# A second buffer for the raw keys of an attention job

## The chip, the cores and the metric

The kernel runs on one core of one Trainium2 chip. The metric is the device time of one execution in microseconds (us), lower is better. Engines of the core are named as the profile names them: PE (TensorE, matrix products; PEld is its weight load), DVE (VectorE), ACT (ScalarE), POOL (GpSimd) and SP (SyncE, which here only issues DMAs; "SPq" marks its DMA instructions). Each engine works through its own list of instructions in order; semaphores hold an instruction back until what it reads is there and what it overwrites is no longer needed.

## What is computed

Three stages follow one another: causal attention with a decay, and two feed-forward layers with a gate of their own kind. Cut to what matters:

```python
def _attn_ref(q, k, v, f):                 # (4, 8, 576, 64), f (4, 8, 576)
    scores = scale * np.matmul(q, k.transpose(0, 1, 3, 2))
    cum = np.cumsum(np.log(np.clip(f, 0.0001, 1.0)), axis=-1)
    decay = cum[:, :, :, None] - cum[:, :, None, :]
    scores = np.where(causal, -1000000000.0, scores + decay)
    ...                                    # softmax over the keys
    return np.matmul(attn, v)

def _moe_ref(x, w_in, w_out):              # 2304 tokens, 512 -> 2048 -> 512
    h = x @ w_in
    return (h * np.clip(h + 3.0, 0.0, 6.0) / 6.0) @ w_out

def _moe2_ref(x, w_in, w_out):
    h = x @ w_in
    g = np.where(h >= 1, h, np.where(h <= -1, 0.0, (h + 1) ** 2 / 4.0))
    return g @ w_out
```

## The kernel before

**Attention** is cut into 64 jobs, 16 for each of the four batches. A pair of heads takes one job for its first 256 queries (a job "two": two heads, two tiles of 128 queries) and three for the remaining 320 (two jobs "one", one head and two tiles each, and a job "last" that takes the last 64 queries of both heads). For each job `u_load` issues its DMAs, `u_split` prepares its operands, `u_scores` makes the scores of a tile on PE and the softmax on DVE and ACT, `u_norm` divides by the row sum, `u_trans` transposes the probabilities on PE (tile `pt`) and `u_out` multiplies with the values (`av`) and writes the result as the first layer's input `xt`.

**The raw keys.** The first eight jobs use keys and queries as they come. From the ninth on (`n >= NATS`) a job of kind "two" or "one" loads its keys into `kraw` (two DMAs, line 259, one for each half of the partitions, the same keys in both) and its queries into `qraw` (lines 264, 272 and 273). `u_split` then makes `kk` from `kraw`: ACT rounds all of it (the helper at line 121) and DVE subtracts the rounded part in the lower 64 partitions (the helper at line 129). In the same way `qraw` becomes `qh` (ACT) and `ql` (DVE). There are 40 such jobs. `kraw` and `qraw` each had one buffer: the next job's DMAs wait until DVE has made `kk` and `ql` of the job before. `kk`, `qh` and `ql` have three buffers each. The decay row `dec` of a job (lines 288 and 239, broadcast from `ncum` in DRAM) has two.

**The feed-forward layers** run over 9 blocks of 256 tokens in the first layer and 5 blocks of up to 512 in the second; for each block 16 chunks of the hidden width. `moe_h` makes `hp` (line 561), ACT and DVE make `u` and from it `g` in two parts (rounded part on ACT at line 121, rest on DVE at line 129), `moe_o` adds to `o` (line 608 in the first layer, 615 in the second). The weights come as pairs of 32-bit words (`wraw`, line 157), are decoded by ACT (line 178) and DVE (lines 179, 183, 186, 189) into `wr`, which has two buffers, and are written to DRAM as `wf` (by POOL's DMA queue, line 194) or split into `w`; `w` is read back from `wf` (line 160).

**Order.** The first layer's steps begin while the attention still runs, and pieces of attention are put between its steps by a table of costs. The program text is not yet the order: the framework's scheduler orders each engine's instructions by a simulation of its own, where a tile's free buffer is one of the conditions, and sets the semaphores. Eight semaphores serve the DMAs of SP in turn, so that a DMA also waits for the one eight places ahead of it.

Of the kernel before, what the change touches and what calls it, by code (L numbers as in the profile page):

```python
# [8 lines left out]
F32 = mybir.dt.float32  # L9
# [5 lines left out]
B, H, S, D = 4, 8, 576, 64  # L15
NT, DM, DFF = B * S, H * D, 2048
P = 128
# [57 lines left out]
def tile_kernel(  # L75
# [34 lines left out]
    att = att_cm.__enter__()  # L110
# [120 lines left out]
    def u_load(n):  # L231
# [13 lines left out]
        if d["nat"]:  # L245

            kk = att.tile([P, S], F32, tag="kk", name="kn", bufs=3)
            qq = att.tile([P, 2 * QA], F32, tag="qh", name="qn", bufs=3)
            nc.sync.dma_start(out=kk[:, 0:nk], in_=k[b, h:h + 2, :, 0:nk].rearrange("h p n -> (h p) n"))
            for y in range(2):  # L250
                nc.sync.dma_start(
                    out=qq[y * D:(y + 1) * D, 0:nq], in_=q[b, h + y, y * D:(y + 1) * D, q0:q0 + nq]
                )
            d.update(kk=kk, qh=qq)
        else:
            kraw = att.tile([P, S], F32, tag="kraw", name="kraw", bufs=1)
            qraw = att.tile([P, 2 * QA], F32, tag="qraw", name="qraw", bufs=1)
            for y in range(2):
                nc.sync.dma_start(
                    out=kraw[y * D:(y + 1) * D, 0:nh * nk].rearrange("p (h n) -> p h n", h=nh),  # L260
                    in_=k[b, h:h + nh, :, 0:nk].rearrange("h p n -> p h n"),
                )
            if kind == "two":
                nc.sync.dma_start(
                    out=qraw.rearrange("p (h n) -> p h n", h=nh),
                    in_=q[b, h:h + nh, :, q0:q0 + nq].rearrange("h p n -> p h n"),
                )
            else:

                o = QA + W4 * (h % 2)  # L270
                nc.gpsimd.memset(qraw[:, S - o:S - o + W4], 0.0)
                nc.sync.dma_start(out=qraw[:, 0:QA], in_=q[b, h, :, q0:q0 + QA])
                nc.sync.dma_start(out=qraw[:, o:o + W4], in_=q[b, h, :, q0 + QA:S])
            d.update(kraw=kraw, qraw=qraw)
# [213 lines left out]
    def attention_pieces():  # L488
# [4 lines left out]
        for n in range(nu + 2):  # L493
            ready = []
            if n < nu:
                d = jobs[n]
                tl = d["tiles"]
                for i in tl:
                    def sc(n=n, i=i, tl=tl):
                        u_scores(n, i)  # L500
                        if i == tl[0] and n + 1 < nu:
                            u_split(n + 1)
                        if i == tl[-1]:
                            u_norm(n)
                            if n + 2 < nu:
                                u_load(n + 2)
                    w = min(i * P + P, S)
                    ready.append(((4 if d["kind"] == "two" else 2) * max(110, w * 0.45), sc))
# [221 lines left out]
    logs(lf)  # L730
    seq, ends = attention_pieces()
    u_load(0)
    u_split(0)
    weights_ahead(-1)
    u_load(1)
    after = cumulative(lf)
    pos = 0
# [112 lines left out]
```

## Time and profile before

| | |
|---|---|
| median of 3 runs | 1085.44 us (1082.84 to 1087.59) |
| the profiled execution | 1085.11 us |
| its span, from the first to the last instruction | 1083.4 us |
| mean granted TensorE clock | 0.974 of full speed |
| busy: PE, PEld | 1034.3 us (95%), 903.9 us (83%) |
| busy: DVE, ACT, POOL | 591.8 us (55%), 541.5 us (50%), 89.8 us (8%) |
| chain that ended last | PE 69%, DMA 15%, DVE 7%, issue 4%, ACT 4% |

Busy time is the time in which an engine executed; the share is that of the span. The attention jobs fill the stretch up to about 560 us, together with the first layer; from then on there are the feed-forward layers alone. In a row of the timeline the first number is the start in us from the span's start, the second how long the instruction (or the run of equal ones) took, and the bracket at the end says how long the engine had been idle ahead of it and what ended that wait.

### The profile page before, as it was taken

The numbers are of one execution on the slowest core, as the hardware profiler recorded it, in microseconds if no ns is written. First come the engines' busy times: TensorE is split into PE (matmuls) and PEld (weight loads), VectorE is DVE, ScalarE is ACT, GpSimd is POOL, SyncE is SP. The second block draws the span as 40 slices with busy tenths as digits, with TensorE's granted clock in tenths as the row PEclk, the third lists the DMA queues.
The fourth block names the chain that finished last, engine by engine and source line by source line (L and its number), as shares of the span: only waits on it lengthen the run. The fifth ranks groups of instructions, "written<-read, shape, count | busy, mean of one in ns | idle before, by whom it ended". The sixth has DMA issues, their size and how long they took to land.

```text
span 1083.4 us, 18101 instructions
## 1 busy us (share of the span) xinstructions
PE 1034.3 (95%) x6556; PEld 903.9 (83%) x6556; DVE 591.8 (55%) x1510; ACT 541.5 (50%) x1330; POOL 89.8 (8%) x223
## 2 busy tenths in 40 slices
PE   7987999989799989999999999999999999999998
PEld 5776989979688889888989999888888888888887
DVE  7999984766577776777653436422422322332232
ACT  6877755656456655556553235533333333333343
POOL 2200010111021111121101000000100100000000
PEclk8688999999999999999999999999999999999999
DMA  8976681783586686864826035200200200010010
GB/s 235 337 222 185 213 299 54 226 277 111 182 282 197 202 298 185 282 212 123 249 68 253 2 96 167 90 1 1 77 1 1 72 6 1 19 39 1 1 40 20
DMA packets 69785, 144.20 MB, mean 133 GB/s; under 512 B 11584, under 2 KB 38720, under 8 KB 65600
## 3 DMA queue, kind: packets, MB, share of 16 engines
q1 hardware_dynamic: 67136, 134.66, 39.6%
q0 software_dynamic: 2560, 8.39, 2.0%
q8 instruction: 51, 0.84, 0.3%
q14 instruction: 38, 0.31, 0.1%
HBM read 116.74 MB, written 26.29 MB: 132 GB/s over the span
## 4 chain that ended last, share of the span: by engine, by line
PE 69%; DMA 15%; DVE 7%; issue 4%; ACT 4%; SPq 1%; POOL 0%; DVEq 0%; ACTq 0%; POOLq 0%
PE hp L561 31%; PE o L608 12%; PE o L615 10%; PE ps L615 8%; DMA qraw<-in_q 5%; DMA dec<-ncum 3%; PE pt L432 3%; DMA kraw<-in_k 2%; PE av L474 2%; DMA wraw<-in_w 2%; PE sc L388 1%; DMA x2d<-osb 1%; DMA wf<-wr 1%; DVE prob L339 1%; DVE wr L186 1%
## 5 line engine op out<-in xcount | busy, mean ns | idle before, releaser
L608 PE MATMUL o<-g,w 128*128 128x256 f32 x1728 | 250.3, 289 | 16.8 <-ACT g L121 15.3
L561 PE MATMUL hp<-xt,w 128*128 128x256 f32 x1728 | 250.6, 292 | 7.8 <-ACT w L121 5.1
L608 PEld LDWEIGHTS o<-g,w 128*128 128x128 f32 x1728 | 225.9, 191 | 26.7 <-ACT g L121 19.2
L561 PEld LDWEIGHTS hp<-xt,w 128*128 128x128 f32 x1728 | 226.8, 194 | 14.5 <-ACT w L121 6.1
L561 PE MATMUL hp<-x,w 128*128 128x512 f32 (+1 forms) x960 | 211.4, 369 | 0.0
L561 PEld LDWEIGHTS hp<-x,w 128*128 128x128 f32 x960 | 169.1, 188 | 32.5
L572 DVE SCALAR_TENSOR_TENSOR u<-hp,u 128x512 f32<-128x512 f32 (+1 forms) x80 | 50.8, 637 | 195.9 <-ACT u L571 195.9
L129 DVE TENSOR_TENSOR g<-u,g 128x256 fp32r<-128x256 f32 (+1 forms) x224 | 112.8, 505 | 71.5 <-ACT g L121 71.1
L121 ACT ACTIVATE g<-u 128x256 fp32r<-128x256 f32 (+1 forms) x224 | 106.1, 475 | 88.4 <-DVE u L572 55.3
L570 ACT ACTIVATE u<-hp 128x512 f32<-128x512 f32 (+1 forms) x80 | 44.6, 557 | 173.3 <-PE hp L561 171.5
L615 PE MATMUL o<-w,g 128*128 128x512 f32 x480 | 125.0, 396 | 0.0
L615 PEld LDWEIGHTS o<-w,g 128*128 128x128 f32 x480 | 89.1, 188 | 19.9
L345 ACT ACTIVATE prob<-prob,mx 128x512 f32<-128x512 f32 (+4 forms) x144 | 83.5, 581 | 37.4 <-DVE mx L339 37.0
L615 PE MATMUL ps<-w,g 128*128 128x512 f32 x384 | 100.4, 396 | 0.0
L568 DVE SCALAR_TENSOR_TENSOR u<-u,hp 128x256 f32<-128x256 f32 x144 | 59.4, 416 | 53.8 <-ACT u L567 53.2
L567 ACT ACTIVATE u<-hp 128x256 f32<-128x256 f32 x144 | 53.8, 378 | 67.2 <-PE hp L561 65.4
L615 PEld LDWEIGHTS ps<-w,g 128*128 128x128 f32 x384 | 72.3, 188 | 17.4
L432 PE MATMUL pt<-ident,prob 128*128 128x128 f32 (+1 forms) x400 | 69.1, 296 | 12.6 <-DVE prob L417 12.1
L339 DVE CUSTOM_DVE_ANT_0 prob<-sc,dec 128x256 f32<-128x256 f32 (+1 forms) x112 | 58.8, 533 | 25.1 <-PE sc L388 11.9
L121 ACT ACTIVATE pt<-pt 128x512 f32<-128x512 f32 (+3 forms) x160 | 61.9, 433 | 18.7 <-PE pt L432 18.2
L432 PEld LDWEIGHTS pt<-ident,prob 128*128 128x128 f32 (+1 forms) x400 | 50.3, 150 | 18.4 <-DVE prob L417 12.8
L178 ACT ACTIVATE wr<-wraw 128x512 f32<-128x512 f32 x64 | 43.0, 671 | 44.5 <-DMA wf<-wr 19.0
(76 smaller groups left out, 975.5 us busy)
## 6 DMA issues: line engine op xcount, KB each, us to landing
wraw<-in_w SPq DMA_DIRECT2D x64, 512.0 KB, 6.4
w<-wf SPq DMA_DIRECT2D x24, 1024.0 KB, 8.5
dec<-ncum SPq DMA_DIRECT2D x45, 256.0 KB, 6.6
kraw<-in_k SPq DMA_DIRECT2D x64, 144.0 KB, 3.8
wf<-w SPq DMA_DIRECT2D x8, 1024.0 KB
wf<-wr POOLq DMA_DIRECT2D x32, 256.0 KB, 6.0
w<-wf SPq DMA_DIRECT2D x16, 512.0 KB, 4.1
vv<-in_v SPq DMA_DIRECT2D x16, 320.0 KB, 10.6
```

The source lines that it names most:

```text
L121: nc.scalar.activation(out=out, in_=in_, func=AF.Copy)
L129: e.tensor_tensor(out=out, in0=in_, in1=hi.bitcast(F32), op=ALU.subtract)
L339: nc.vector.tensor_tensor_reduce(out=py[:, a:e], in0=s, in1=dc, scale=-0.125, scalar=mx[:, 2 * z:2 * z + 1] if x else 3.0e38, op0=ALU.add, ...
L345: nc.scalar.activation(out=py, in_=py, func=AF.Exp, scale=-1.0, bias=mx[:, 2 * z + x:2 * z + x + 1], accum_out=sm[:, z:z + 1],)
L432: nc.tensor.transpose(t[:nk, o:o + P], p[:, c:c + nk], ident)
L561: nc.tensor.matmul(hp, lhsT=ws[:, a, k], rhs=x[:, bb, 0:w], start=(k == 0 and a == 0 and bb == 0), stop=(k == KD - 1 and bb == 1),)
L567: nc.scalar.activation(out=u, in_=hp, func=AF.Relu, bias=3.0, scale=1.0)
L568: nc.vector.scalar_tensor_tensor(out=u, in0=u, scalar=6.0, in1=hp, op0=ALU.min, op1=ALU.mult)
L570: nc.scalar.activation(out=u, in_=hp, func=AF.Relu, bias=0.5, scale=0.5)
L572: nc.vector.scalar_tensor_tensor(out=u, in0=hp, scalar=1.0, in1=u, op0=ALU.max, op1=ALU.min)
L608: nc.tensor.matmul(o, lhsT=ws[:, a, KD + k], rhs=gg[:, bb], start=False, stop=(n == NCH - 1 and bb == 1 and k % 2 == 1),)
L615: nc.tensor.matmul(acc[j][k], lhsT=gg[:, bb, k * P:(k + 1) * P], rhs=ws[:, a, KD:2 * KD].rearrange("p k n -> p (k n)"), start=(n == 0 and ...
```

## The change

One number: `kraw` gets two buffers in the pool `att` instead of one, 2304 bytes more in each partition.

```diff
-            kraw = att.tile([P, S], F32, tag="kraw", name="kraw", bufs=1)
+            kraw = att.tile([P, S], F32, tag="kraw", name="kraw", bufs=2)
             qraw = att.tile([P, 2 * QA], F32, tag="qraw", name="qraw", bufs=1)
```

No instruction is added or taken away. The scheduler, which sees the free buffer, puts the instructions of SP, ACT, DVE and PE into another order. The first difference on SP lies in the first 20 us, on ACT and DVE at the eighth job with raw keys, on PE some 200 us into the span. In the rows that follow, a line with + stands in the new program alone, one with - in the old alone, and a number behind a name tells one buffer's use from another's.

The first place is the loads of two neighbouring jobs "one", about 450 to 470 us into the span before. On SP (`kraw_6613` with `qraw_6614` is a job's load, `kraw_6656` with `qraw_6657` the next job's, `kraw_6935` that of the job after):

```order
 L273 DMA qraw_6614<-in_q 128x64
-L157 DMA wraw_6944<-in_w 128x1024
-L259 DMA kraw_6613<-in_k 64x576
+L259 DMA kraw_6656<-in_k 64x576 x2
+L259 DMA kraw_6935<-in_k 64x576
 L160 DMA w3_118<-wf15_97 128x2048
-L259 DMA kraw_6613<-in_k 64x576
+L259 DMA kraw_6935<-in_k 64x576
 L157 DMA wraw_6946<-in_w 128x1024
+L157 DMA wraw_7226<-in_w 128x1024
+L239 DMA dec_6445<-ncum_114 128x1x576
 L272 DMA qraw_6657<-in_q 128x256
```

The keys of each job stand one job earlier in SP's queue, and the decay row `dec_6445` now stands ahead of the next job's queries.

On DVE at the same place (`ql_6645` belongs to the queries `qraw_6614`, `wr_6865` to a weight chunk, `prob1_6434` is the last reader of the buffer into which `dec_6445` is loaded):

```order
-L129 TENSOR_TENSOR ql_6645<-qraw_6614,qh_6644 128x384
+L186 SCALAR_TENSOR_TENSOR wr_6865<-wraw_6683,wr_6865 128x512
+L189 SCALAR_TENSOR_TENSOR wr_6865<-wraw_6683,wr_6865 128x512
 L339 ISA prob1_6434,mx_6308<-sc_6435,dec_6277 128x256
 L339 ISA mx_6308 128x1
-L179 TENSOR_SCALAR wr_6865<-wr_6865 128x512
 L568 SCALAR_TENSOR_TENSOR u_6425<-u_6425,hp_6412 128x256
 L339 ISA prob0_6459,mx_6400<-sc_6460,dec_6320 128x256
 L339 ISA mx_6400 128x1
-L183 TENSOR_SCALAR wr_6865<-wr_6865 128x512
+L129 TENSOR_TENSOR ql_6645<-qraw_6614,qh_6644 128x384
```

The split of the queries has moved from ahead of `prob1_6434` to behind it, and the weight steps of `wr_6865` have moved ahead.

The second place is DVE some 15 us later, between the softmax of the job "last" and the two divisions (line 417) whose results PE transposes next:

```order
-L179 TENSOR_SCALAR wr_7175<-wr_7175 128x512
+L129 TENSOR_TENSOR kk_6726<-kraw_6656,kk_6726 64x576
+L186 SCALAR_TENSOR_TENSOR wr_7175<-wraw_6944,wr_7175 128x512
+L129 TENSOR_TENSOR kk_6988<-kraw_6935,kk_6988 64x576
 L408 RECIPROCAL rd_6608<-sum_6399 128x2
-L129 TENSOR_TENSOR kk_6726<-kraw_6656,kk_6726 64x576
-L183 TENSOR_SCALAR wr_7175<-wr_7175 128x512
+L568 SCALAR_TENSOR_TENSOR u_6700<-u_6700,hp_6687 128x256
+L189 SCALAR_TENSOR_TENSOR wr_7175<-wraw_6944,wr_7175 128x512
+L408 RECIPROCAL rd_6652<-sum_6473 128x1
+L179 TENSOR_SCALAR wr_7182<-wr_7182 128x512
 L417 TENSOR_SCALAR prob0_6459<-prob0_6459,rd_6608 128x384
```

Two keys' splits instead of one, both steps of the weight decoding and `u_6700` now stand ahead of the divisions.

The third place is ACT about 456 us into the span, where a row sum (`sum_6045`) is needed by the next divisions:

```order
 L121 ACTIVATE kk_6392<-kraw_6313 128x576
 L178 ACTIVATE wr_6576<-wraw_6410 128x512
+L121 ACTIVATE kk_6643<-kraw_6613 128x576
 L407 ACTIVATE sum_6045<-sum_6045 128x2
```

The rounding of the next job's keys, which stood some twenty instructions further on, now stands ahead of the row sum. At eleven places ACT now rounds two jobs' keys one directly behind the other, where before it never did.

## Rows read from the trace of the kernel before

**Rows 1.** Busy time by stretch: us, busy (x count), PEclk, DMA share, GB/s

```profile
216.00:560.00 344.00, 323.02 (x2449) 292.19 (x2449) 239.27 (x712) 200.52 (x571) 51.59 (x138) 0.98 0.66 210
560.00:680.00 120.00, 120.00 (x967) 115.43 (x964) 55.20 (x113) 47.78 (x107) 5.68 (x10) 1.00 0.37 125
```

**Rows 2.** PE's waits, 216 to 560 us: total us, times, longest

```profile
PE pt L432 <- DVE prob L417: 10.2, 6, 3.6
PE o L608 <- ACT g L121: 6.6, 5, 2.8
```

**Rows 3.** ACT's waits for raw queries and keys, whole span: total, times, longest

```profile
ACT qh L121 <- DMA qraw<-in_q: 20.2, 10, 3.4
...
ACT kk L121 <- DMA kraw<-in_k: 14.7, 9, 4.4
```

**Rows 4.** Instructions on tile kraw: count, duration in ns min/median/max

```profile
L259 SPq DMA_DIRECT2D kraw<-in_k x80: 465/587/1231, 14.4 to 542.4; - x80
L121 ACT ACTIVATE kk<-kraw x40: 615/674/702, 39.6 to 551.6; 128x576 fp32r<-128x576 f32 x32, 128x512 fp32r<-128x512 f32 x8
L129 DVE TENSOR_TENSOR kk<-kraw,kk x40: 689/755/841, 41.0 to 552.4; 64x576 fp32r<-64x576 f32 x32, 64x512 fp32r<-64x512 f32 x8
```

**Rows 5.** Timeline of DVE, ACT and PE, 478 to 484 us

```profile
478.57 0.69 DVE L339 CUSTOM_DVE_ANT_0 prob<-sc,dec 128x512 f32<-128x512 f32 x1 [2.29 <-DMA dec<-ncum]
...
481.55 0.68 ACT L121 ACTIVATE kk<-kraw 128x576 fp32r<-128x576 f32 x1 [4.40 <-DMA kraw<-in_k]
...
482.27 0.76 DVE L129 TENSOR_TENSOR kk<-kraw,kk 64x576 fp32r<-64x576 f32 x1 [1.57 <-ACT kk L121]
...
483.40 0.81 DVE L417 TENSOR_SCALAR prob<-prob,rd 128x384 f32<-128x384 f32 x2
...
483.87 0.44 PE L432 MATMUL pt<-ident,prob 128*128 128x128 f32 x2 [2.27 <-DVE prob L417]
```

**Rows 6.** Busy time by stretch, just behind that stall (columns as in rows 1)

```profile
485.00:488.40 3.40, 3.40 (x17) 3.36 (x16) 3.37 (x9) 2.48 (x7) 1.52 (x4) 0.51 0.24 79
```

**Rows 7.** Timeline of DVE and SP, 464 to 467 us

```profile
464.93 0.56 DVE L129 TENSOR_TENSOR ql<-qraw,qh 128x384 fp32r<-128x384 f32 x1 [3.80 <-ACT qh L121]
465.41 0.69 DVE L339 CUSTOM_DVE_ANT_0 prob<-sc,dec 128x512 f32<-128x512 f32 x1
...
466.37 0.55 SPq L239 DMA_DIRECT2D dec<-ncum  x1
```

**Rows 8.** DVE's weight steps by line, whole span: busy us, mean ns

```profile
L189 DVE SCALAR_TENSOR_TENSOR wr<-wraw,wr 128x512 int32<-128x512 int32 x64 | 44.3, 692 | 0.4
L186 DVE SCALAR_TENSOR_TENSOR wr<-wraw,wr 128x512 int32<-128x512 int32 x64 | 43.8, 686 | 0.2
...
L183 DVE TENSOR_SCALAR wr<-wr 128x512 int32<-128x512 int32 x64 | 27.3, 427 | 0.5
```

**Rows 9.** Timeline of ACT and PE, 353 to 355 us

```profile
353.35 0.63 ACT L121 ACTIVATE kk<-kraw 128x512 fp32r<-128x512 f32 x1 [0.65 <-DMA kraw<-in_k]
...
354.93 0.51 PE L561 MATMUL hp<-xt,w 128*128 128x256 f32 x2 [0.85 <-ACT xt L121]
```

**Rows 10.** Timeline of ACT and PE, 455 to 458 us

```profile
455.58 0.66 ACT L178 ACTIVATE wr<-wraw 128x512 f32<-128x512 f32 x1 [5.16 <-DMA wf<-wr]
...
457.54 0.54 PE L432 MATMUL pt<-ident,prob 128*128 128x128 f32 x2 [2.70 <-DVE prob L417]
```

**Rows 11.** Timeline of ACT and PE, 293 to 297 us

```profile
293.87 0.66 ACT L178 ACTIVATE wr<-wraw 128x512 f32<-128x512 f32 x1 [2.72 <-DMA wf<-wr]
...
296.82 0.44 PE L432 MATMUL pt<-ident,prob 128*128 128x128 f32 x2 [3.57 <-DVE prob L417]
```

**Rows 12.** Timeline of DVE and PE, 401 to 406 us

```profile
401.68 0.69 DVE L339 CUSTOM_DVE_ANT_0 prob<-sc,dec 128x512 f32<-128x512 f32 x1 [3.14 <-DMA dec<-ncum]
...
406.00 0.79 PE L608 MATMUL o<-g,w 128*128 128x256 f32 x4 [2.31 <-ACT g L121]
```

**Rows 13.** Busy time by stretch, 20 us ahead of that (columns as in rows 1)

```profile
382.00:388.00 6.00, 5.78 (x46) 5.20 (x45) 5.18 (x19) 4.26 (x12) 0.11 (x1) 1.00 1.03 416
```

**Rows 14.** The chain of waits in order of time, the start: us, duration

```profile
16.41 4.52 DMA kn<-in_k
```

## The prediction, made before the changed kernel was run

> **What bounds the kernel now.** I read the stretches first, then who waits for whom, then the timeline at each long wait of PE. In all stretches it is PE that works: behind 560 us it does not wait at all for 120 us [rows 1], and attention is over by then, so only what happens ahead of 560 us can answer to this change. From 216 to 560 us PE is busy for 323.0 of 344 us [rows 1]; 21.0 us are idle, and two kinds of wait make most of them: transposes that wait for the softmax division on DVE (10.2 us) and second products that wait for `g` from ACT (6.6 us) [rows 2]. No wait of PE names the raw keys. They show one step further up: ACT waits for the keys' DMA nine times, 14.7 us in all, and for the queries' DMA ten times, 20.2 us in all [rows 3]. So queries, which keep their one buffer, are late more often than keys. What a wait of ACT is worth depends on whether PE runs dry behind it. The reader should go through the long stalls with that question.
>
> There are five of 2.2 us or more behind 216 us (the others are under 1.8 us). One has the keys on its way: ACT waits 4.40 us for them, DVE 1.57 us for ACT, and PE 2.27 us for the division that stands behind on DVE [rows 5]. Two are ended by a decoded weight's buffer: ACT waits 2.72 and 5.16 us for the DMA that writes it away, and PE 3.57 and 2.70 us [rows 10, 11] (the fifth, at 224 us, is of that kind too, and I leave it as it is). In one DVE waits 3.14 us for the decay row and PE 2.31 us [rows 12]. Behind the stall at 483.87 us the granted clock is 0.51 for 3.4 us, that is the 1.2 GHz level instead of 2.4 [rows 6]; half of the work of 3.4 us is lost, 1.7 us. I take the same for each of the five long stalls: such a stall costs its length and 1.7 us.
>
> **The change, part by part.** Nothing is added on any engine, so the busy sums stay; all cost and gain is in the order. The keys of a job are loaded one job earlier, and the sum goes by places.
>
> *The stall at 483.87 us.* The keys' DMA (`kraw_6656`) now stands behind the queries of the job before, so it is issued when the other buffer is free, at about 452 us, and the wait of 4.40 us [rows 5] goes. What is late next is the decay row: DVE had waited 2.29 us for it, until 478.57 [rows 5]. Its issue at 466.37 follows the last reader of its buffer, which began at 465.41 behind the split of the queries, and that split had kept DVE idle for 3.80 us [rows 7]. In the new order the split stands behind the reader. Into the idle time go four weight steps, 0.69 + 0.69 + 2 x 0.43 = 2.2 us [rows 8], so 1.6 us are left, and the split's own 0.5 us goes from the reader's way: the decay row is issued 2.1 us earlier, and I let it land as much earlier. From its landing to the end of the wait for the division DVE took 483.40 - 478.57 = 4.83 us [rows 5]. Of that go 1.57 us of idleness and one weight step (0.43); new are a second keys' split (0.75 [rows 4]), two weight steps (1.38 [rows 8]) and three small steps that I take as one more 0.75. Steps that follow each other overlap by nearly 0.1 us each, 0.5 in all. That makes 4.83 - 2.0 + 2.9 - 0.5 = 5.2 us, 0.4 more than before. The division is ready 2.1 - 0.4 = 1.7 us earlier, and the stall is 0.6 us. I take 1.0, since the decay row may land less early than it is issued: 1.3 us gained, and 1.7 of clock, since stalls under 1.8 us left the clock as it was: **-3.0**. The bounds are -4.0 (all of it goes) and +0.4 (the decay row lands as late as before, and the stall grows by what is new on DVE).
>
> *The wait at 354.93 us.* ACT waits 0.65 us for keys, then PE 0.85 us [rows 9]. The keys are there earlier, the rest stays: **-0.65**, between -0.85 and 0.
>
> *The stall at 457.54 us.* The next job's keys are now rounded on ACT (0.67) and split on DVE (0.75) [rows 4] between the weight that is late [rows 10] and the row sum and divisions that PE waits for. One runs on ACT while DVE has its own weight step, so not all counts: **+1.0**, between 0 and 0.67 + 0.75 = 1.4.
>
> *The stalls at 296.82 and 406.00 us.* Their ends, a weight's buffer and a decay row [rows 11, 12], are not moved: the decay row at 406 us stands behind another job's keys in the same places of SP's queue. In the second, keys' splits again come in between. **+0.3** each, between 0 and 0.75. Ahead of the latter the DMA engines are busy all the time (share 1.03) and move 416 GB/s [rows 13], so keys brought in there earlier push something else back. The Trainium skill, DMA: Bandwidth & Descriptors, section Where 436 GB/s comes from, gives 435 GB/s as the ceiling of a core's transfers; by it a second buffer can only trade places in such stretches, and the stall would be the same to the tenth.
>
> *The start.* The keys of the second such job now go out some 25 us earlier, the first half of them directly ahead of a weight and of the keys (`kn`) whose DMA lies on the chain, 4.52 us from 16.41 [rows 14]. The price is SP's time for two more DMAs, 2 x 0.59 = 1.2 us [rows 4], at most; it comes back at 43 us where they are no longer, but some of it passes on: **+0.6**, between 0 and 1.2.
>
> *The other places.* At eleven places ACT has two keys' roundings in a row. Each takes the same time earlier instead of later; where ACT and DVE have idle time ahead (they are busy for 200.5 and 239.3 of 344 us [rows 1]), this costs nothing. If that cover is gone, each costs up to 0.75. I take 0 here; the rest is the last rival.
>
> Sum: -3.0 - 0.65 + 1.0 + 0.6 + 0.6 = -1.45 us. Against the profiled execution, 1085.11 us (its span of 1083.4 and 1.7 around it), that is 1083.7; the median of the runs is 0.33 higher, so **1084 us**.
>
> **Rivals.** *Keys were not what held it up (no gain).* Queries have one buffer and wait longer [rows 3]; the next division is as late as before. Then the first term is 0 instead of -3.0: 1087 us. For it: the new work on DVE ahead of the division is as long as the idleness that goes. Against it: the decay row's earlier issue. Chance 0.22.
>
> *Faster.* Keys leave SP's queue and ACT's waits, what stood behind them goes out earlier, and three long stalls go with their clock: 2.27 + 2.31 + 2.70 [rows 5, 10, 12] + 3 x 1.7 = 12.4 us, 1073 us. For it: SP works in order, and the keys stood ahead of decay rows. Against it: the weights' buffers do not change. The Trainium skill, Trainium Kernel Development and Optimization, section Best Practices, has double buffering as a rule for overlapping DMA with compute; by that rule all nine waits for keys end, and the trace agrees only in so far as ACT has these nine waits. Chance 0.20.
>
> *Slower.* Keys' splits that come too early: at the eleven places the second one (0.75 on DVE [rows 4]) stands ahead of a division or a `g` that PE waits for. 11 x 0.75 = 8.2, and one more long stall drops the clock for 1.7 more: 1095 us. It decides from the point at which DVE has less than 0.75 us of idle time ahead of the work PE needs; in long stalls [rows 5, 10, 12] that is so already, elsewhere the 105 us of DVE's idle time in the stretch [rows 1] speak against it. Chance 0.21.
>
> **How the numbers follow.** The forecast, 1084 with 1080 to 1088 as its own range, has 0.37. A measurement of this kernel can tell a change of about 0.5% (5.4 us) from none. Faster than 1080.0: the faster rival and a little of the forecast's lower end, 0.24. Slower than 1090.9: most of the slower rival and the upper end of the first, 0.20. Between them 0.56. The range reaches to the middle of both outer rivals, 1074 to 1095, and leaves out some 0.1 on each side.
>
> **What would show it.** Right: ACT's waits for keys fall from 14.7 us to a few, those for queries stay near 20; around 480 us a stall of PE under 1.8 us and no clock drop behind it; the stall at 457 us about 1 us longer; PE's idle time from 216 to 560 us between 18 and 21 us. Wrong: the stall at 483.87 stays, with DVE busy instead of idle ahead of it (first rival); idle time under 12 us and two or three clock drops less (second); new waits of PE for divisions where two keys' splits stand in a row (third). If keys become late again on ACT, two buffers do not do what they say.

## The result: 0.83% slower

| | before | changed |
|---|---|---|
| median of 5 runs | 1085.44 us (1080.8 to 1087.59) | 1092.44 us (1091.5 to 1095.85) |
| ratio | 1 | 1.0083, 95% interval 1.0060 to 1.0107 |
| profiled execution, its span | 1085.11 us, 1083.4 | 1091.5 us, 1089.8 |
| mean granted clock | 0.974 | 0.971 |

The forecast was 1084 us, 1.4 less than before; the kernel became 7.0 us slower instead, outside the forecast's own range of 1080 to 1088 us, though inside the wide one of 1074 to 1095 us. The second buffer does what it says: ACT no longer waits for raw keys anywhere, where it had waited 14.7 us in nine waits [rows 3]. Its waits for queries have grown instead from 20.2 to 26.6 us, those for write-outs from 19.0 to 24.1 us, and PE's idle time has grown too. The first group is the changed kernel's busy time from 216 to 560 us (columns as in rows 1), the second its PE's waits there (as rows 2), the third ACT's waits for queries and for a weight's write-out over the whole span (as rows 3).

```profile
216.00:560.00 344.00, 317.85 (x2390) 287.92 (x2389) 235.27 (x691) 195.95 (x555) 48.65 (x136) 0.96 0.66 208
...
PE o L608 <- ACT g L121: 13.1, 6, 3.0
...
PE pt L432 <- DVE prob L417: 8.6, 4, 4.7
...
ACT qh L121 <- DMA qraw<-in_q: 26.6, 14, 3.4
ACT wr L178 <- DMA wf<-wr: 24.1, 8, 6.0
```

PE is idle for 344.00 - 317.85 = 26.2 us against 21.0 [rows 1]. The new part is in second products that wait for `g`: 13.1 us against 6.6 [rows 2]. The granted clock is at its lower level for 27 us of the stretch (0.96 on average) against 17 us before; at half speed that is another 5 us lost. Added up that is 26.2 - 21.0 + 5 = 10 us, but the two overlap, since PE is also idle inside windows of low clock; and by 40 us this execution is 1.1 us ahead. What is left is the 6.4 us by which the span is longer.

The timelines show where. The first place is the one with the stall at 457 us before [rows 10], in the changed kernel at 465 us: ACT, DVE and PE.

```profile
462.02 0.66 ACT L178 ACTIVATE wr<-wraw 128x512 f32<-128x512 f32 x1 [5.04 <-DMA wf<-wr]
462.58 0.67 ACT L121 ACTIVATE kk<-kraw 128x576 fp32r<-128x576 f32 x1
463.15 0.19 ACT L407 ACTIVATE sum<-sum 128x2 f32<-128x2 f32 x1
...
463.28 0.76 DVE L129 TENSOR_TENSOR kk<-kraw,kk 64x576 fp32r<-64x576 f32 x1
...
464.47 0.81 DVE L417 TENSOR_SCALAR prob<-prob,rd 128x384 f32<-128x384 f32 x2
...
464.94 0.69 PE L432 MATMUL pt<-ident,prob 128*128 128x128 f32 x2 [4.68 <-DVE prob L417]
```

From ACT's weight step to PE's transposes it was 457.54 - 455.58 = 1.96 us before [rows 10] and is 2.92 us now, since the next job's keys stand between the weight and the row sum, as forecast (+1.0). The stall has grown by 2.0 us, to 4.68, so another microsecond came from elsewhere.

The second place is the one at which I had forecast the gain [rows 5], in the changed kernel at 490 to 493 us, and the third lies at 248 us, where before had a stall of 0.46 us only:

```profile
490.32 0.66 ACT L178 ACTIVATE wr<-wraw 128x512 f32<-128x512 f32 x1 [1.37 <-DMA wf<-wr]
...
491.79 0.52 ACT L121 ACTIVATE qh<-qraw 128x384 fp32r<-128x384 f32 x1 [0.80 <-DMA qraw<-in_q]
492.21 0.40 ACT L121 ACTIVATE g<-u 128x256 fp32r<-128x256 f32 x1
...
492.67 0.74 PE L608 MATMUL o<-g,w 128*128 128x256 f32 x4 [3.03 <-ACT g L121]
...
248.08 0.52 ACT L121 ACTIVATE qh<-qraw 128x384 fp32r<-128x384 f32 x1 [3.36 <-DMA qraw<-in_q]
248.51 0.40 ACT L121 ACTIVATE g<-u 128x256 fp32r<-128x256 f32 x1
...
248.96 0.74 PE L608 MATMUL o<-g,w 128*128 128x256 f32 x4 [1.74 <-ACT g L121]
```

Neither of the two has keys in it. A rounding of queries, and a weight step, each waiting for a DMA, stand ahead of the `g` that PE waits for, which they did not in the order before. The clock also drops at 286 us, behind a stall of 2.35 us (1.77 before, without a drop), and at 327 us, behind three stalls of 1.23, 0.48 and 1.28 us within 6 us, which before does not have. So there were three suspects: **A**, the keys' roundings and splits that now come early, in pairs; **B**, the rest of the order, which the scheduler made anew; **C**, the traffic of loads that go out earlier.

### The profile page after: what moved, and what is told of

Its sections match the earlier page's. It is cut to its first block, busy times and chain, and to the rows that moved or that the text cites. A ratio compares the mean times of both kernels' runs of the same rounds, so it can differ in the third digit from the quotient of the medians.

```text
span 1089.8 us, 18108 instructions
## 1 busy us (share of the span) xinstructions
PE 1036.0 (95%) x6556; PEld 906.8 (83%) x6556; DVE 593.6 (54%) x1510; ACT 542.0 (50%) x1330; POOL 87.8 (8%) x223
## 2 busy tenths in 40 slices
DMA packets 69785, 144.20 MB, mean 132 GB/s; under 512 B 11584, under 2 KB 38720, under 8 KB 65600
## 4 chain that ended last, share of the span: by engine, by line
PE 71%; DMA 15%; DVE 7%; issue 3%; ACT 2%; SPq 1%; POOL 0%; DVEq 0%; ACTq 0%; POOLq 0%
PE hp L561 31%; PE o L608 12%; PE o L615 10%; PE ps L615 8%; DMA dec<-ncum 6%; DMA qraw<-in_q 4%; PE av L474 3%; PE pt L432 3%; DMA wf<-wr 2%; PE sc L388 2%; DVE prob L339 1%; PE sc L363 1%; DMA wraw<-in_w 1%; DMA x2d<-osb 1%; DVE wr L186 1%
## 5 line engine op out<-in xcount | busy, mean ns | idle before, releaser
L345 ACT ACTIVATE prob<-prob,mx 128x384 f32<-128x384 f32 (+4 forms) x144 | 83.6, 581 | 38.5 <-DVE mx L339 37.9
L615 PEld LDWEIGHTS ps<-w,g 128*128 128x128 f32 x384 | 72.3, 188 | 17.4
L178 ACT ACTIVATE wr<-wraw 128x512 f32<-128x512 f32 x64 | 42.9, 670 | 49.3 <-DMA wf<-wr 24.1
```

Source lines behind the costliest of these rows:

```text
L345: nc.scalar.activation(out=py, in_=py, func=AF.Exp, scale=-1.0, bias=mx[:, 2 * z + x:2 * z + x + 1], accum_out=sm[:, z:z + 1],)
L615: nc.tensor.matmul(acc[j][k], lhsT=gg[:, bb, k * P:(k + 1) * P], rhs=ws[:, a, KD:2 * KD].rearrange("p k n -> p (k n)"), start=(n == 0 and ...
```

## The experiments

Each kernel was measured beside fresh runs of the kernel before, whose medians lay between 1083.13 and 1084.75 us; the ratio is to those, and so is not the median over 1085.44 us.

| kernel | median, us | ratio to before, 95% interval |
|---|---|---|
| one buffer, tiles moved by 2304 bytes | 1084.80 | 1.0012 (0.9995 to 1.0029) |
| two buffers, key steps tied behind query steps | 1098.23 | 1.0132 (1.0112 to 1.0152) |
| one buffer, the same tie | 1084.86 | 1.0002 (0.9982 to 1.0021) |
| two buffers for queries, one for keys | 1099.90 | 1.0147 (1.0127 to 1.0168) |
| two buffers, order of before | 1081.85 | 0.9983 (0.9962 to 1.0003) |
| ... but the keys as in the changed kernel | 1086.67 | 1.0015 (0.9993 to 1.0038) |
| two buffers, new order, the keys as before | 1097.76 | 1.0127 (1.0111 to 1.0143) |
| one buffer, new order | 1180.50 | 1.0885 (1.0848 to 1.0923) |
| changed kernel, one instruction moved | 1093.74 | 1.0084 (1.0057 to 1.0112) |
| changed kernel, three places mended | 1088.96 | 1.0042 (1.0024 to 1.0060) |
| before, the three places spoilt | 1085.11 | 1.0018 (1.0002 to 1.0034) |
| four buffers for `kk` | 1086.74 | 1.0023 (1.0009 to 1.0036) |
| four buffers for `qh` | 1114.71 | 1.0271 (1.0240 to 1.0301) |
| two buffers, order of before, 3 weight steps moved | 1084.43 | 1.0007 (0.9992 to 1.0021) |
| ... 4 places, further back | 1083.92 | 0.9988 (0.9972 to 1.0004) |
| ... and 4 places ahead of 110 us | 1083.69 | 0.9996 (0.9979 to 1.0012) |
| two buffers, order of before, small decay loads | 1049.61 | 0.9683 (0.9657 to 0.9709) |
| the one with 4 places, small decay loads | 1049.91 | 0.9692 (0.9669 to 0.9716) |

### Are the pairs of key steps the cost?

First a control. The new buffer also moves the tiles behind it:

```diff
     jobs, pairs = [], []
+    pad = att.tile([P, S], F32, tag="pad", name="pad", bufs=1)
+    nc.gpsimd.memset(pad[:, 0:1], 0.0)
```

> The kernel before (one buffer for raw keys) with a tile of 2304 bytes per partition in the same pool that nothing reads, so that the tiles behind it lie where they lie in the changed kernel; the order on every engine stays that of before. Theory A (key roundings in pairs ahead of a division or of ACT's g) and theory B (any other place at which the order differs) both expect 1085 us, within 2 of before, with PE's idle time of 216 to 560 us near 21.0 us. If the place of the tiles in SBUF costs the 7 us, this one has them too: 1092 us.

Measured 1084.80 us, no difference: places in SBUF are out. Then the changed kernel without its pairs, by ties of issue order:

```diff
-                rounded("a", kk[:, 0:w], kraw[:, 0:w])
-                rest("v", kk[D:P, 0:w], kraw[D:P, 0:w], kk[D:P, 0:w])
-                rounded("a", qh[:, 0:x], qraw[:, 0:x])
-                rest("v", ql[:, 0:x], qraw[:, 0:x], qh[:, 0:x])
+                h_ = rounded("a", qh[:, 0:x], qraw[:, 0:x])
+                l_ = rest("v", ql[:, 0:x], qraw[:, 0:x], qh[:, 0:x])
+                with tc.issue_after(h_.ins):
+                    rounded("a", kk[:, 0:w], kraw[:, 0:w])
+                with tc.issue_after(l_.ins):
+                    rest("v", kk[D:P, 0:w], kraw[D:P, 0:w], kk[D:P, 0:w])
```

> The changed kernel (two buffers for raw keys), but each key rounding of ACT is held behind the query rounding of the same step, and each key split of VectorE behind that step's query split. No two key roundings stand in a row any more on either engine, and SP no longer issues four key loads in a row. Theory A (the pairs are the cost): the 7 us come back, 1084 to 1086 us, PE's idle time of 216 to 560 us near 21 us, and no stall over 2.5 us for a division or for g that before does not have. Theory B (the order is only another one, and each new order has its own stalls): anything from 1080 to 1095 us, with stalls at other places. Theory C (a second set of raw keys in flight takes the DMA engines from queries and decays): half of it or more stays, 1089 us or above, unless the loads are no longer issued earlier than in before.

> The kernel before (one buffer for raw keys) with the same holding back of key roundings and key splits. It is the control of the tied kernel with two buffers: the tie itself should cost nothing, 1084 to 1087 us, since in before a key rounding already comes behind the query rounding at nearly every step. The difference between the two tied kernels is then what a second buffer is worth when it makes no pairs. Theory A: within 2 us of each other. If queries gate all the same (my second case of the prediction), also within 2 us.

The tie costs nothing with one buffer (1084.86), and with two the kernel has no pair left, yet takes 1098.23 us, 6 us more than the changed kernel and more than theories A and B had allowed. Theory A fails as I had put it: pairs aren't needed for the loss. The mirror image, two buffers for queries (`bufs=2` for `qraw` instead):

> The kernel before with two buffers for a job's raw queries and one for its raw keys: the mirror image. ACT's wait for queries (20.2 us in 10 waits in before) should go, and query roundings now stand in pairs at ten places, in one case of five of SP's with query loads in a row. Theory A, taken as a rule for any pair of roundings (a query rounding of 384 columns is shorter than a key rounding of 576): a loss of some 3 to 5 us, 1088 to 1090 us. If it is the keys' pairs alone that hurt: 1083 to 1086 us. If the wait for queries was what bounded: below 1080 us.

It took 1099.90 us, more than any theory expected. The wait for queries goes as meant, but ACT's waits for keys double, from 14.7 to 31.7 us.

### The order held fixed

The scheduler's order can be taken out of the question. Neither kernel has an instruction that the other lacks, so a stored list of one kernel's order can be imposed on the other:

```diff
     with tile.TileContext(nc, schedule_with_timeline_sim=True) as tc:
         tile_kernel(tc, *args)
+        pinned(tc)
...
+def pinned(tc):
...
+    for names in stored.values():
+        row = [traced[f"I-{n}"] for n in names if f"I-{n}" in traced]
+        for a, b in zip(row, row[1:]):
+            tc.add_manual_dep(b, a.name, how, reason="pinned")
```

Each edge only says that an instruction is issued behind the one ahead of it in the list. PE, DVE, ACT and POOL are held so; SP stays free to issue loads as early as the buffers let it. With two buffers that gives four kernels: the order of the key steps old or new, the order of all the rest old or new (both new is the changed kernel as it is, not held; held with one instruction moved it gave 1.0084, so holding by itself costs nothing that shows).

> Two buffers for raw keys, but TensorE, VectorE, ScalarE and GpSimd are each held to the order of the kernel before, instruction by instruction; SyncE alone is left to issue the key loads as early as the second buffer lets it. Theory A (key roundings and splits taken early stand ahead of divisions and g) and theory B (it is the order of everything else that got worse) both expect that the loss is gone, 1080 to 1086 us, and the part below 1085 is what the second buffer saves by itself, as my forecast had it (1084). Theory C (the earlier loads cost by their traffic): 1088 us or more. ACT's wait for keys, 14.7 us in 9 waits of 216 to 570 us in before, should fall below 5 us.

> Two buffers; all four engines held to the order of before, except that the key roundings of ACT and the key splits of VectorE stand where the changed kernel has them (the second key of a pair 4 to 20 ACT instructions earlier, eleven pairs on ACT and six on VectorE). Theory A: the loss of the changed kernel is here, 1089 to 1094 us, with PE's waits for divisions and for g at 405 and 460 us longer than before by 1 to 2 us each. Theory B: no more than 1086 us. If part of it: between them, and the rest should show in the kernel with the opposite mixture.

> Two buffers; all four engines held to the order of the changed kernel, except that the key roundings and key splits stand where before has them, behind the same instruction: no pairs. Theory A: 1083 to 1086 us, the loss is gone. Theory B (the order of the rest): 1090 us or more, as in the tied kernel with two buffers (1098) whose order has no pairs either.

| | key steps as before | key steps as in the changed kernel |
|---|---|---|
| rest as before | 0.9983 | 1.0015 |
| rest as in the changed kernel | 1.0127 | 1.0083 |

With all of the old order the loss is gone, and the second buffer by itself is worth 0.17%, with an interval that reaches zero. The early key steps alone cost 0.32%, some 3.5 us, for the pairs on ACT, eleven as counted in the program (the changed kernel's trace shows twelve; the two intervals overlap a little): suspect A is small at most, and in the new order the same steps even help by 0.4%. The rest of the new order costs 1.4% with old key steps and 0.7% with new ones. Suspect B carries most of the loss. Suspect C, the early loads, is out as the main cost: all four have the second buffer and SP free to use it, ACT waits for no raw key in the best of them, and it is no slower than before. The fourth kernel of the set shows how far the new order relies on its buffer:

> One buffer for raw keys, and the four engines held to the order of the changed kernel. Both key roundings of a pair now stand together with one buffer between them, so the second waits for a load that can start only when the first split is done: at eleven places some 3.5 to 5 us (load and split) on ACT. If the order of the changed kernel is what costs, whatever the buffers: above 1092 us, and with those waits on the path at even a third of the places, 1100 to 1120 us. If it comes out near 1085 the order is harmless and the cost lies in the second buffer itself.

1180.50 us, beyond what I expected: with the second load bound to wait for the first split, the new order costs 8.9%.

### Mending the places, and spoiling them

> The changed kernel, every engine held to its order there, with one VectorE instruction moved: near 405 us a softmax piece that waits 4.3 us for its decays stands ahead of two divisions that TensorE waits for; here it stands behind them, as in before. Theory B in its sharper form (an instruction that waits for a DMA now stands ahead of the division or of the g that TensorE needs): the stall of 1.80 us at 407 goes, and one of the two low-clock windows behind it (half of 3.4 us): 1088.5 to 1090.5 us. If the order of the rest works in some other way: 1092, no difference.

> The same with two more places mended: near 248 us ACT's query rounding, which waits 3.4 us for its load, stands behind the g that TensorE waits for (1.74 us there), its query split behind VectorE's g; near 490 us ACT's g stands ahead of the weights' rounding and the query rounding that wait for DMAs (TensorE waits 3.03 us there). Sharper theory B: 1.7, 1.8 and 3.0 us of stalls, with what the clock gives back 5 to 8 us: 1084.5 to 1087.5 us. If stalls only move on to the next late thing: above 1089 us.

> The counterpart: the kernel before, one buffer for raw keys, every engine held to its order there, with the same three places spoilt as the changed kernel has them: the softmax piece that waits for decays ahead of the divisions, the query roundings ahead of g, and at 490 us the weights' rounding too. Sharper theory B: slower by 2 to 6 us, 1086 to 1090 us, without any second buffer. If the places matter only in the changed kernel's other order: 1083 to 1086 us.

The edit of the second one on ACT, as rows of the order (the DVE steps that belong to them moved too, and on DVE at 405 us a softmax piece behind two divisions, which alone is the edit of the first):

```
-L121 ACTIVATE qh<-qraw 128x384
-L121 ACTIVATE g<-u 128x256
+L121 ACTIVATE g<-u 128x256
+L121 ACTIVATE qh<-qraw 128x384
...
-L178 ACTIVATE wr<-wraw 128x512
-L121 ACTIVATE qh<-qraw 128x384
-L121 ACTIVATE g<-u 128x256
+L121 ACTIVATE g<-u 128x256
+L178 ACTIVATE wr<-wraw 128x512
+L121 ACTIVATE qh<-qraw 128x384
```

At 405 us the move gained nothing (1093.74): the stall of 1.80 us stayed as long as it was; the one of 1.93 us behind it shrank to 0.72, but the clock is low for 10.2 us there instead of 6.8. With all three places the ratio falls from 1.0083 to 1.0042 (1.0024 to 1.0060), about half of the loss. In its profile the stall at 248 us is gone, and the low clock behind 405 and 457 us is down from 13.6 to 3.4 us (the second of these places was not edited, and its stall fell from 4.68 to 3.25 us all the same); but up to 482.85 and 487.00 us PE waits for 1.55 + 2.27 = 3.8 us in two stalls where it had waited for 3.03 in one, so that place was not mended. And since the move at 405 us alone gives nothing, which place gave the half is not settled. Spoiling the same places in the kernel before costs 0.18%, the lower end of what was expected. So a place costs what it does only in its surroundings, and the loss is spread over more than these three.

### Is any new order as bad?

If so, a buffer that nobody waits for should cost as well. For a buffer of `kk` ACT waits only once in the trace of before, 0.3 us at 53 us (the expectation below has it as no wait); for one of `qh` it waits 2.2 us in four waits.

```diff
-                kk = att.tile([P, S], F32R, tag="kk", name="kk", bufs=3)
+                kk = att.tile([P, S], F32R, tag="kk", name="kk", bufs=4)
...
-                qh = att.tile([P, 2 * QA], F32R, tag="qh", name="qh", bufs=3)
+                qh = att.tile([P, 2 * QA], F32R, tag="qh", name="qh", bufs=4)
```

(one of the two in each kernel, with the same number for the keys or queries of the first eight jobs)

> The kernel before with one raw buffer, and a fourth buffer for the split keys kk (2304 bytes per partition, as much as the change adds), for which no engine waits in the trace of before: there is no wait that it could remove. The scheduler's order changes all the same (some 130 rows on PE, 220 on VectorE, 150 on ACT, counted as half the lines of difference). If any new order of the scheduler costs here, whatever the buffer is for (theory B as order luck): 1089 to 1100 us. If it takes a second set of raw operands to lose: 1083 to 1086 us.

> The kernel before with one raw buffer and a fourth buffer for the rounded queries qh, for which ACT waits 2.2 us in 4 waits of 40 to 570 us in before. The order changes more (twice the rows of the fourth key buffer). Order luck: 1089 to 1105 us. If the buffers for finished operands are harmless: 1081 to 1086 us.

The fourth `kk` buffer costs 0.23%, less than expected, the fourth `qh` buffer 2.7%, 30 us. Every kernel whose order the scheduler made anew for another buffer is slower than before: by 0.2, 0.8, 1.3, 1.5 and 2.7%. The two whose order stayed that of before are not, within what a measurement tells (0.9983 with the second buffer, 1.0012 with the tiles moved). The kernel before has, of these six orders, the one that came out best; the changed kernel's loss lies in the middle of the five. Only for the changed kernel were buffer and order taken apart; for the other four, that it is the order is argued from their likeness to it.

### What the late thing is

Then it should be possible to mend the order of before too. In the kernel with two buffers and that order three stalls of PE stand behind a weight step on ACT that waits for a write-out, as in [rows 10, 11]; the step was moved behind what PE waits for.

> Two buffers, before's order on the four engines (1081.85 us), and three weights' roundings that wait 6.2, 2.7 and 6.3 us on ACT for a write-out moved behind what TensorE waits for: at 221 us behind the exponential, g and the sum, at 293 and 456 us behind the sum, and on VectorE behind g or the divisions. Sharper theory B, turned into a gain: the stalls of 2.41, 3.55 and 3.80 us go in whole or half, and with them three low-clock windows of 3.4 us at half speed (1.7 us each): 1068 to 1076 us. If another wait ends last at those places, or the weights' later roundings make the next chunk late: 1078 to 1084 us.

> Two buffers, before's order on the four engines, as the kernel that came out at 1081.85 us; weights' roundings that wait for a write-out are moved further back than in the first attempt: at 221, 293 and 456 us, and on VectorE too, behind the exponential, the sum, the divisions and g of that step, so that the next stall (1.7, 1.7 and 2.1 us in the first attempt) goes as well; at 283 us one of them stands behind ACT's and VectorE's rounding of the attention output, for which TensorE waits 1.9 us. If what stands ahead of the releaser is the cost at these four places: 1070 to 1077 us. If the next stall takes its place once more: 1080 to 1085 us.

> The same, and before 110 us four places of the same kind: near 85 us a query split and a key split of VectorE (0.69 us each) moved behind the weight part that TensorE waits 4.2 us for, and near 69, 77 and 102 us VectorE's u and ACT's g moved ahead of weight work (TensorE waits 2.15, 2.00 and 2.34 us there). Worth 1.4, 0.7, 0.6 and 1.4 us by the rows, 3 to 5 us together with what the clock gives back, below the kernel beside it. If other waits take their place: no difference to it.

The ACT part of the last edit at 456 us:

```
 L121 ACTIVATE kk<-kraw 128x576
-L178 ACTIVATE wr<-wraw 128x512
 L407 ACTIVATE sum<-sum 128x2
...
 L121 ACTIVATE g<-u 128x256
+L178 ACTIVATE wr<-wraw 128x512
```

Nothing came of it: 1084.43, 1083.92 and 1083.69 us. The stalls did go where they had been, and stood elsewhere within 10 us. These are stalls of PE in the second of these kernels, and two lines of who waits for a load there, 216 to 560 us:

```profile
226.48 0.69 PE L388 MATMUL sc<-kk,qh 128*128 128x384 f32 x1 [3.23 <-ACT pt L121]
...
300.71 0.47 PE L388 MATMUL sc<-kk,qh 128*128 128x512 f32 x1 [3.46 <-DVE mx L339]
...
299.62 0.42 DVE L339 CUSTOM_DVE_ANT_0 prob<-sc,dec 128x256 f32<-128x256 f32 x1 [2.00 <-DMA dec<-ncum]
...
ACT qh L121 <- DMA qraw<-in_q: 20.6, 10, 5.2
DVE prob L339 <- DMA dec<-ncum: 17.2, 9, 4.5
```

DVE's wait for decays was 10.4 us in before in the same stretch. And there is a far longer wait that I had not used, since POOL is busy for only 8% of the span: POOL masks a job's decays (lines 302 and 315) and waits for their load each time. In before, 216 to 570 us:

```profile
POOL dm L302 <- DMA dec<-ncum: 134.0, 13, 12.7
POOL dm L315 <- DMA dec<-ncum: 65.4, 24, 7.7
```

What stands behind POOL's mask are the write-outs `wf` (line 194) for which ACT's weight steps wait, and the memset of `qraw` behind which the queries' load stands. (In the kernel with two buffers and the order of before, 17 of the 24 memsets in this stretch come out of a wait for DVE's split of the job before, so POOL's queue can have held seven at most.) One chain, followed in the kernel with two buffers and the order of before, SP to PE:

```profile
439.50 0.54 SPq L239 DMA_DIRECT2D dec<-ncum  x1
...
443.61 0.68 DVE L189 SCALAR_TENSOR_TENSOR wr<-wraw,wr 128x512 int32<-128x512 int32 x1
...
450.69 0.56 POOL L302 TENSOR_SCALAR_AFFINE_SELECT dm<-dec 128x64 f32<-128x64 f32 x1 [9.76 <-DMA dec<-ncum]
451.32 0.23 POOL L306 TENSOR_SCALAR_AFFINE_SELECT dm<-dec 64x64 f32<-64x64 f32 x1
451.80 0.56 POOL L194 DMA_DIRECT2D wf<-wr  x1 [0.24 <-DVE mx L339]
...
453.13 0.54 POOL L194 DMA_DIRECT2D wf<-wr  x1 [0.61 <-DVE wr L189]
...
458.34 0.66 ACT L178 ACTIVATE wr<-wraw 128x512 f32<-128x512 f32 x1 [6.27 <-DMA wf<-wr]
458.90 0.19 ACT L407 ACTIVATE sum<-sum 128x2 f32<-128x2 f32 x1
...
460.30 0.63 PE L432 MATMUL pt<-ident,prob 128*128 128x128 f32 x2 [3.81 <-DVE prob L417]
```

The decays take 11 us from issue to POOL's mask. The weights were ready at 444.3 us, but their write-out goes out only behind the mask, at 451.80 us (the one at 453.13 is the next chunk's). ACT, which reuses that buffer, waits for it, the row sum stands behind ACT's wait, and PE behind the division. The largest new stall of the tied kernel has the same chain with longer links: POOL's wait 16.10 us, ACT's 9.26, PE's 5.50. But it is not the chain of every such stall. Ahead of the longest one of before, at 296.82 us [rows 11]:

```profile
282.91 0.66 ACT L178 ACTIVATE wr<-wraw 128x512 f32<-128x512 f32 x1 [6.52 <-DMA x2d<-osb]
...
286.42 0.68 DVE L189 SCALAR_TENSOR_TENSOR wr<-wraw,wr 128x512 int32<-128x512 int32 x1
...
287.40 0.56 POOL L194 DMA_DIRECT2D wf<-wr  x1 [4.57 <-DVE wr L189]
```

Here POOL had been waiting for the weights for 4.57 us, and the write-out left 0.3 us behind DVE's last step. What was late is ACT's weight step, behind a wait of 6.52 us that the profile puts down to the write of `x2d`.

If the decays are at the root of all this, small decay loads must take the stalls away, in whichever order:

```diff
+    def decays(n):
+        if n < 2:
+            kept.append(att.tile([P, S], F32, tag=f"dec{n}", name="dec", bufs=1))
+            return kept[n]
...
+        return kept[n % 2]
...
-                out=dec[:, 0:nh * w].rearrange("p (h n) -> p h n", h=nh),
-                in_=ncum[r:r + nh, 0:w].unsqueeze(0).to_broadcast([P, nh, w]),
+                out=dec[:, 0:nh * w].rearrange("p (h n) -> p h n", h=nh)[:, :, 0:w if n < FULL else 16],
+                in_=ncum[r:r + nh, 0:w if n < FULL else 16].unsqueeze(0).to_broadcast([P, nh, w if n < FULL else 16]),
```

(`FULL` is 18; the load of the job "last" is cut in the same way)

> The kernel with two buffers in before's order (1081.85 us), with the decays' loads from the 19th job on (some 215 us) cut to 16 of 256 to 576 columns into two tiles that are kept, so that the other columns hold an earlier job's decays; the order on the four engines is the same. It leaves out data and shows what that wait is worth. Theory D (the decays' loads end last where TensorE stalls, whatever the keys do): 1074 to 1079 us, and VectorE's and GpSimd's waits for decays mostly gone. If it is the write-outs of weights that end last, or if those waits come from the reuse of the two buffers: 1080 to 1083 us.

> The same cut in the kernel whose weights' roundings were moved behind the releasers at four places (1083.92 us). Theory D: with the decays there, those moves should at last pay, 1068 to 1075 us, some 5 us below the kernel beside it. If a further wait (queries, which ACT waited 20.6 us for, or the weights themselves) takes the place: equal to the kernel beside it within 2 us.

1049.61 and 1049.91 us, 32 and 34 us less than the same orders with full loads, far more than theory D as I had sized it. Busy time of the first from 216 to 560 us, and its POOL and ACT waits for decays, queries and write-outs there (its line numbers behind 210 are 10 higher):

```profile
216.00:560.00 344.00, 344.00 (x2723) 315.80 (x2722) 251.18 (x741) 216.13 (x608) 58.23 (x145) 1.00 0.61 196
...
POOL dm L325 <- DMA dec<-ncum: 6.2, 3, 2.4
ACT qh L121 <- DMA qraw<-in_q: 4.3, 6, 1.3
ACT wr L178 <- DMA wf<-wr: 3.2, 2, 1.8
```

PE does not wait at all from 216 to 560 us, and its clock stays at the upper level. With the decays' wait most of the waits for queries (17.4 us with full loads) and for write-outs (19.6 us) have gone too. The sum fits about: with full loads PE is idle for 344.00 - 321.52 = 22.5 us there, and 17 us at half speed lose 8.5 more, 31 us. Moving the weight steps is now worth nothing, since no stall is left for it.

But the edit does more than shorten the loads. POOL's masks of the jobs "one" and "last" read columns 256 to 576, and the loads now write only columns 0 to 15, so these masks no longer wait for their load at all. There are 16 jobs "last", and the last of their masks comes ahead of the last of their loads:

```profile
522.06 0.24 POOL L312 TENSOR_SCALAR_AFFINE_SELECT dm<-dec 128x64 f32<-128x64 f32 x1 [3.61 <-DVE mx L349]
...
523.76 0.53 SPq L249 DMA_DIRECT2D dec<-ncum  x1
```

The three waits for decays that POOL's masks have left belong to jobs "two", whose mask does read loaded columns. So the 32 us are what the decays cost altogether, and not what a faster load would give. What these two runs don't tell apart is how much lies in the masks that no longer wait, how much in the time that a load takes to land (median 6.8 us, now 3.2 for the 42 smallest), and how much in the 144.20 - 132.09 = 12 MB that the DMA engines no longer move (`wraw` lands in 5.8 instead of 7.0 us; the wait of 6.52 us above is 0.17 us). Both runs have the order of before, or that with four places moved: whether small loads would bring the changed kernel's order to the same time, and so whether decays are also what makes a new order dear, was not run. A third buffer for decays, which would let the full loads go out earlier, was not tried.

## Why the prediction was wrong

**What bounds the kernel** was read one step short. PE's stalls end with divisions and `g`, as said, and one was traced back to the keys, two to write-outs, one to decays [rows 5, 10 to 12]. The write-outs were taken as causes of their own; the one behind the stall at 457.54 us was late because POOL's queue stood behind the decays (the one at 296.82 us was not, it left as soon as its weights were there). POOL's 134.0 us of waiting for decays were in the trace and stood in no step. The Trainium skill, PSUM — Partial Sum Buffer, section Engine vs sequencer instructions, says that the queues of ScalarE, VectorE and GpSimdE are strictly first in, first out; the trace agrees: a POOL wait of 9.76 us holds back a write-out that has nothing to do with decays, from 444.3 us, when its weights were ready, to 451.80.

**The stall at 483.87 us (-3.0)** gave 0.9 us instead of 3.0. ACT's wait for keys did go, and a stall of 3.03 us instead of 2.27 is there all the same, now for `g` behind a weight step and queries. The clock drop behind it went, as forecast, though not for the reason given, a short stall. In the order of before the second buffer shortens that stall to 0.76 us: the term's mechanism was right for the buffer, and the scheduler's new order took it away.

**The wait at 354.93 us (-0.65)** went as forecast. **The stall at 457.54 us (+1.0):** the key steps between weight and division cost 0.96 us, as forecast; the stall grew by 2.0, and the low clock behind it doubled from 3.4 to 6.8 us, which had no term: 3.7 us in all. **The stalls at 296.82 and 406.00 us (+0.3 each):** the first shrank from 3.57 to 2.92 us, and is now a wait for `g`; for the second there are two, 1.80 and 1.93 us, with 6.8 us of low clock, 3.1 us more. That stalls under 1.8 us leave the clock as it was held in the trace of before, and does not hold in this one: it fell at 327 us behind stalls of 1.23, 0.48 and 1.28 us. **The start (+0.6)** came out as a gain of 1.1 us by the profiled execution, but that can't be told from chance: the stall of 2.3 us that stands at 103.66 us in before and at 102.54 in the changed kernel stands at 103.74 and at 102.33 in two kernels with the order of before (tiles moved; three places spoilt).

**The other places (0)** is the step that failed, and by which the sign was lost. It priced pairs of key steps alone. The pairs cost 3.5 us where all else is as before, 0.3 us each where I had written up to 0.75 without cover; so the third rival had the sign and its mechanism, and a share of it. But the program differs from before at hundreds of rows without keys, and those I held to cost nothing, without a reason. They cost 0.7 to 1.4%, 7 to 16 us. Which of them cost what is open: three places mended gave back half.

**The rivals.** The first, that keys were not what held it up, is what the buffer by itself shows: 0.17% (-0.03 to 0.38), with queries and decays waited for as before. Its price of 1087 us took the order as given. The second needed decays and write-outs to come earlier, which did not happen; its stalls were the right ones, and with the decays cut, all stalls together were worth more than its 12.4 us. The Trainium skill's rule from Trainium Kernel Development and Optimization, section Best Practices, to double-buffer for overlap, is kept to the letter by the change; the measurement differs: all nine waits ended, at most 0.4% came of it.

**What I said would show it:** the keys' waits fell to none; the queries' rose to 26.6 us instead of staying near 20; PE's idle time was to be 18 to 21 us and was 26.2. The sign that I had set for the third rival, new waits where two splits stand in a row, was seen at 465 us only.

## What to carry to other kernels

Where a scheduler orders the instructions, a change of one buffer is two changes, the buffer and a new order: hold the old order fixed to price the first, and try a buffer that hardly anyone waits for to see what a new order costs. Follow a stall past the instruction that ended it to what that one's queue stood behind, also on an engine that is hardly busy: here POOL, busy for 8%, held back write-outs and by them ACT, DVE and PE. Before buying a buffer, cut the suspected load to a few columns once: that shows in one run what the load costs altogether, its traffic with it. Look in the trace whether its readers still wait for it; where they no longer do, the figure is an upper bound for a faster load.

## What the runs showed of the hardware that was not expected

Waits for different loads were not independent: cutting the decays' loads alone took ACT's waits for queries from 17.4 to 4.3 us and for write-outs from 19.6 to 3.2 us. And removing stalls one by one gave nothing while the full decay loads stood: mending the weight steps at three, four and eight places gave nothing that could be measured, cutting the decays' loads 3.2%. With small decay loads and no stall over 0.5 us from 150 to 1045 us, the clock stayed at its upper level. From 216 to 560 us it fell behind all five stalls of 2 us or more in before and behind four of five in the changed kernel, though not behind the one of 3.03 us at 493 us, nor behind one of 3.25 us at 460 us in the kernel with three places mended; and it fell at 327 us in the changed kernel behind stalls of 1.23, 0.48 and 1.28 us alone.
